# Mirrored sums and differences in a two-dimensional Fourier transform beside attention, one core of a Trainium2

## The chip, the cores and the metric

One core of one Trainium2 chip. The metric is the device time of one execution in microseconds; the kernel before was run three times. The core's engines are called PE (TensorE, matrix multiplication), ACT (ScalarE), DVE (VectorE), POOL (GpSimd) and SP (SyncE, which issues nearly all transfers here). They run side by side, each through its own fixed list of instructions in order, and wait for one another by semaphores. PSUM, where PE leaves its results, has eight banks.

## The reference

```python
B, S, D = 1, 2048, 448;  H = 16;  Dh = 28
g = sigmoid((x * gate_w).sum(-1))
qkv = x @ wqkv
p = softmax(q k^T * Dh ** -0.5)            # 16 heads, 2048 x 2048 each
a = (p v) @ wo
X = rfft2(x)                               # 2048 x 225 complex
b = irfft2(X * (w_r + 1j * w_i))
return g * a + (1 - g) * b
```

Both halves read the same x; everything is in bfloat16 outside, sums are in float32.

## The kernel before, in words

**Attention.** The 16 heads make four groups G of four. A group's queries are cut into four chunks of 512, so there are 16 chunks (CHUNKS gives their order). A chunk has 16 *packs*: one key tile of 128 keys, 512 queries, four heads. A pack's four units are scores of 128x512, each one matmul with a contraction of 32 (rows of the array, one strip a head). Two ways lead from scores to probabilities:

- ACT takes two units at a time from two-bank tiles psA and psB and writes exp into P, a ring of 20 units (line 901). The first few packs go into VS instead.
- DVE takes a unit from a psX bank and makes the bits of a bfloat16 power of two out of it by an addition in int16 (line 930). The result is a coarse exponential. From it DVE makes three more versions with other offsets (line 936), and all four are multiplied with the values, so that their errors cancel. Such a pack has four value products instead of one.

A value product is four matmuls side by side, each on 32 columns of the array, added up in psV over a whole chunk. When a chunk is done, DVE empties psV (line 1512) and the next opens.

**Fourier part.** `fft1` (lines 1380 to 1396) transforms over 128 rows: for each of 16 row tiles t and four column blocks c of 112, one matmul with the tokens as weights and R1 (128 columns) as the moving operand; four such fill a bank, DVE evicts it into U (line 1393). `fft2` (lines 1415 to 1470) does the rest for 16 blocks g of frequencies: f2 multiplies U with Bd, the cosine and sine table over the 448 columns of x (four blocks c of 112, each 452 columns wide, added up in one bank); f3 applies the twiddle table; POOL multiplies with the filter; i1 begins the way back. `fft3` does i2, `final` adds both halves. Bd's tile is reused for wo afterwards (line 1028). All these matmuls, and the projections, are cut by `mmc` into 32-column pieces that run side by side; only `fft1` and the transposes use the whole array.

**Order.** No engine's order is written out by hand. `Plan` is a small simulation in the program that builds the kernel: each operation has an engine, a cost and what it depends on, and `pe_step` (line 640) picks at each moment what PE does next by a score. Scores for ACT come first; other work is taken if it fits before ACT needs its next tile. Work of the Fourier part is offered in *units*, each with a time from which it may start and a time at which it is due, counted in chunks. `claim` (line 539) gives a pack to DVE when a bank, a free slot in VS and DVE's backlog allow it. So the number of packs that go to DVE comes out of the plan. If PE's work in the last 3.413 us, counted in columns (`load`), falls under z_hard, dense work is favoured or matmuls with zeros are put in (`zero`). An operation with port=True is one that the plan doesn't let POOL and DVE do at once. CFG holds the weights of all these choices, with one set of changes for each of 18 stretches: 16 chunks and what comes after (line 853); `run` looks up the set by `progress` (line 297).

Of the kernel before, what the change touches and what calls it, by code (L numbers as in the profile page):

```python
# [18 lines left out]
FP = F + 1  # L19
NG, NC = 4, 4  # L20
C = 112
# [20 lines left out]
def rfft_tables():  # L42
# [43 lines left out]
    bd = Bd.reshape(NC, C, 2 * FP).transpose(1, 0, 2)  # L86
# [72 lines left out]
class Plan:  # L159
# [116 lines left out]
    def run(self):  # L276
# [563 lines left out]
    def unit_run(self, u, o, t):  # L840
# [5 lines left out]

CFG = dict(
# [6 lines left out]
        0: dict(d_open=4, w_hungry=0, z_hard=3550, w_open=1.2),  # L854
        1: dict(tol=0),
        3: dict(tol=0.15),
        4: dict(ahead=2, tol=0.15),
        5: dict(v2_due=3.1, hungry=4, w_pv=0.6, tol=0.15),
        6: dict(hungry=4, prio_shift=3, tol=0.15),
        7: dict(w_pv=0.6, tol=0, v2_at=0.5, prio_shift=3),  # L860
        8: dict(w_pv=0.6, tol=0, prio_shift=3, z_hard=3550),
        9: dict(d_urg=1, d_chunks=0, w_due=4, prio_shift=3, z_hard=3550),
        10: dict(z_hard=3550, d_open=4),
        11: dict(z_hard=3550, g_at=[1.1, 4.3, 8.0]),
        12: dict(d_urg=1, ring_urg=8, z_hard=3550),
        13: dict(ring_urg=4, w_pv=0.2, prio_shift=3, z_hard=3550, d_urg=1, w_new=2.0, z_soft=3800, w_late=2),
        14: dict(w_open=0.2, prio_shift=3.5, ahead=1, w_late=2, w_pv=0.2, ring_urg=4, w_new=2.0, w_due=4, pv_min=2, z_soft=3800),
# [75 lines left out]
class Kernel:  # L943
# [36 lines left out]
    def tiles(self, ctx):  # L980
# [26 lines left out]
        self.R1T = self.cst[:, 460:588]  # L1007
# [101 lines left out]
    def loads(self):  # L1109
# [16 lines left out]
        self.d_r1 = self.dma(self.cst[:, 332:588], cs[:, 332:588], 5.0, [self.d_wv])  # L1126
        self.d_bd = self.dma(self.Bd[0:C, :, :], self.c_bd.ap(), 4.0, [self.d_r1])
# [252 lines left out]
    def fft1(self):  # L1380
        nc = self.nc
        self.o_u = []
        i = 0
        for tq in range(4):
            for c in range(NC):
# [7 lines left out]
                self.o_u.append(u.use("DVE", 0.61, lambda bank, e, c=c, tq=tq: nc.vector.tensor_copy(  # L1393
                    out=self.U[0:C, c, :, 4 * tq:4 * tq + 4, :],
                    in_=bank[0:C, :].rearrange("p (t g e) -> p g t e", t=4, g=NT))))
# [19 lines left out]
    def fft2(self):  # L1415
# [5 lines left out]
        for g in range(NT):  # L1421
# [4 lines left out]
            for c in range(NC):  # L1426
                u.mm(lambda bank, c=c, g=g: self.mmc(bank[:, 0:452], self.U[0:C, c, g, :, :].rearrange("p t e -> p (t e)"), self.Bd[0:C, c, :], c == 0, c == NC - 1), n=452, kind="bg", eff=0.875, deps=self.o_u + [self.d_bd])
# [182 lines left out]
```

## Time and profile before

| | us |
|---|---|
| median of three runs | 400.09 |
| lowest and highest | 399.91, 401.86 |
| the profiled execution | 400.49 |
| its span, first to last instruction | 398.7 |
| ACT, PE, DVE, POOL busy | 383.6, 386.0, 344.3, 126.9 |

The profile is one execution. A group's row gives line, engine, operation, what it writes and reads (partitions x elements), how often, then the busy time, the mean ns of one, and the engine's idle time before them with what ended it. Instructions of one engine overlap: the next can start before the last has ended, so the distance of two starts says more than the duration. A timeline row gives start, duration, and the instruction.

### The profile page before, as it was taken

Reading aid. Unit: us, or ns where it says so; the run is one execution under the profiler, and the core shown is the slowest. Engines: PE = TensorE matmul, PEld = TensorE weight load, DVE = VectorE, ACT = ScalarE, POOL = GpSimd, SP = SyncE. Lnnn points to the kernel's source line nnn. Section 1 sums busy time; section 2 is a strip of 40 time slices with the busy share of each in tenths; the row PEclk is TensorE's granted clock in tenths of the full one; section 3 lists DMA queues with packets and bytes.
Section 4 is the critical chain, followed back from the end, with each engine's and each line's share of the span. In section 5 each row is a group of like instructions: output and inputs, shape, how many; then the busy total and the mean of one; then the engine's idle time right before and its main releaser. Section 6 shows DMA issues by size and latency. Waiting matters only on the chain.

```text
span 398.7 us, 12653 instructions
## 1 busy us (share of the span) xinstructions
PE 386.0 (97%) x5221; PEld 134.9 (34%) x5221; DVE 344.3 (86%) x622; ACT 383.6 (96%) x424; POOL 126.9 (32%) x176
## 2 busy tenths in 40 slices
PE   8999999999999999999999999999999999999996
PEld 4444332223333322332332333333334332323233
DVE  3668999988887897898799797799998999999992
ACT  4898999999999999999999999999999999999993
POOL 1044214432333135525444534542436720101010
PEclk9999999999999999999999999999999999999999
DMA  8800022000121102120130112012100100001012
GB/s 250 181 31 5 2 28 58 13 19 3 37 70 34 40 3 66 32 77 20 24 100 19 56 37 58 14 42 74 36 29 2 29 3 25 30 27 50 26 53 71
DMA packets 24394, 17.69 MB, mean 44 GB/s; under 512 B 15731, under 2 KB 19744, under 8 KB 24336
## 3 DMA queue, kind: packets, MB, share of 16 engines
q1 hardware_dynamic: 23728, 16.69, 15.7%
q8 instruction: 41, 0.67, 0.7%
q10 hardware_dynamic: 608, 0.19, 0.3%
q14 instruction: 17, 0.14, 0.1%
HBM read 14.71 MB, written 1.97 MB: 42 GB/s over the span
## 4 chain that ended last, share of the span: by engine, by line
PE 46%; ACT 44%; issue 8%; DMA 1%; DVE 1%; ACTq 0%; DVEq 0%
ACT P L901 44%; PE psX L952 16%; PE psV L952 13%; PE psB L952 8%; PE psA L952 8%; DMA xtok<-in_A_x_dram 1%; PE psX L1202 1%; ACT VS L901 0%; DVE KT L1246 0%; DVE QT L1246 0%; ACT Vb L1227 0%; DVE Vb L1348 0%; PE psV L1202 0%; ACT sq L1556 0%; ACT sq L1237 0%
## 5 line engine op out<-in xcount | busy, mean ns | idle before, releaser
L901 ACT ACTIVATE P<-psB 128x1024 bf16<-128x1024 f32 x198 | 219.9, 1110 | 0.0
L901 ACT ACTIVATE P<-psA 128x1024 bf16<-128x1024 f32 x198 | 219.6, 1109 | 0.1
L930 DVE TENSOR_SCALAR VS<-psX 128x512 int16<-128x512 f32 x212 | 138.9, 681 | 17.3 <-PE psX L952 16.4
L936 DVE TENSOR_SCALAR VS<-VS 128x2048 int16<-128x2048 int16 x159 | 101.5, 689 | 0.4
L952 PEld LDWEIGHTS <-KT 32*128 32x128 bf16 (+1 forms) x1040 | 47.8, 91 | 145.3 <-issue 141.0
L952 PE MATMUL psB<-QT,KT 32*128 32x512 bf16 x406 | 79.2, 382 | 6.3 <-ACT P L901 5.0
L952 PE MATMUL psA<-QT,KT 32*128 32x512 bf16 x406 | 79.6, 383 | 0.9 <-DVE QT L1246 0.6
L952 PE MATMUL psV<-VS,Vb 128*32 128x512 bf16 x868 | 76.0, 385 | 0.1
L952 PE MATMUL psV<-P,Vb 128*32 128x512 bf16 x792 | 73.7, 385 | 0.0
L952 PE MATMUL psX<-QT,KT 32*128 32x512 bf16 x212 | 70.4, 383 | 0.0
L952 PEld LDWEIGHTS <-Vb 128*32 128x32 bf16 x1660 | 33.3, 94 | 57.0 <-issue 51.9
L1441 POOL TENSOR_TENSOR t<-FX,Wf 128x452 bf16<-128x452 f32 x32 | 31.8, 1013 | 56.1 <-PE psX L952 26.3
L1521 POOL TENSOR_TENSOR xtok<-osb,RB 128x512 bf16<-128x512 f32 x12 | 15.3, 1274 | 61.8 <-DMA RB<-rgd 47.6
L1184 POOL TENSOR_TENSOR sq<-QT 128x512 bf16<-128x512 bf16 x16 | 16.6, 1040 | 42.9 <-DVE QT L1266 17.3
L1495 POOL TENSOR_TENSOR UZ<-tab 128x225 bf16<-128x225 f32 (+1 forms) x32 | 17.7, 583 | 21.0 <-DVE VS L936 14.7
L952 PE MATMUL psX<-xT,Wk 112*32 112x512 bf16 x256 | 20.5, 383 | 0.0
L952 PE MATMUL psX<-xT,Wq 112*32 112x512 bf16 x240 | 20.0, 383 | 0.0
L1184 POOL TENSOR_TENSOR sq<-KT 128x512 bf16<-128x512 bf16 x12 | 12.5, 1040 | 22.6 <-DVE KT L1174 17.1
L952 PE MATMUL psX<-Bd,UZ 112*32 112x452 bf16 x256 | 19.6, 358 | 0.0
L1449 POOL TENSOR_TENSOR t<-t,t 128x226 bf16<-128x226 bf16 x32 | 17.9, 584 | 5.0 <-DVE VS L936 4.3
L952 PE MATMUL psX<-Wv,xT 112*32 112x113 bf16 (+1 forms) x512 | 19.4, 262 | 0.0
L952 PEld LDWEIGHTS <-xT 112*32 112x32 bf16 (+1 forms) x576 | 10.5, 96 | 9.0 <-issue 7.0
(105 smaller groups left out, 301.5 us busy)
## 6 DMA issues: line engine op xcount, KB each, us to landing
tab<-c_tab SPq DMA_DIRECT2D x16, 256.0 KB
RB<-rgd SPq DMA_DIRECT2D x60, 64.0 KB
xtok<-in_A_x_dram SPq DMA_DIRECT2D x4, 448.0 KB
out_dram<-ost SPq DMA_DIRECT2D x6, 224.0 KB
rs<-osb SPq DMA_DIRECT2D x60, 2.0 KB
Wf<-in_B_w_r_dram SPq DMA_DIRECT2D x31, 28.1 KB
Wf<-in_B_w_i_dram SPq DMA_DIRECT2D x31, 28.1 KB
Qf<-in_A_wqkv_dram SPq DMA_DIRECT2D x2, 294.0 KB
```

The costliest lines, as they stand in the source:

```text
L901: k.nc.scalar.activation(out=out, in_=k.psS[e["grp"]][:, 0:n, :], func=ACT.Exp, scale=LN2_128)
L930: k.nc.vector.tensor_scalar(out=k.VS[:, slot, 512 * h:512 * h + 512], in0=bank, scalar1=float(BITS0), scalar2=BITS_MIN, op0=ALU.add, op1=A ...
L936: k.nc.vector.tensor_scalar(out=k.VS[:, dst, :], in0=k.VS[:, src, :], scalar1=float(SHIFTS[v - 1]), scalar2=None, op0=ALU.add)
L952: self.nc.tensor.matmul(out, lhsT=lhsT, rhs=rhs, start=start, stop=stop, skip_group_check=True, **kw)
L1184: (self.nc.vector if e == "DVE" else self.nc.gpsimd).tensor_tensor(out=sq[:, :], in0=src, in1=src, op=ALU.mult)
L1202: nc.tensor.transpose(out=bb[0:C, 512 * ci + 128 * k:512 * ci + 128 * k + 128], in_=self.xtok3[:, 4 * b + k, C * c:C * c + C], identity=se ...
L1441: ts.append(pl.op("POOL", 1.07, lambda e, i=i, q=q: nc.gpsimd.tensor_tensor(out=self.t12[i][q][:, :].rearrange("p (r f) -> p r f", r=2), i ...
L1449: (nc.vector if e == "DVE" else nc.gpsimd).tensor_tensor(out=t1[:, FP * q:FP * q + FP], in0=t1[:, FP * q:FP * q + FP], in1=t2[:, FP - FP * ...
L1495: nc.gpsimd.tensor_tensor(out=z, in0=a, in1=b, op=ALU.subtract if q else ALU.add)
L1521: prev = pl.op("POOL", 1.3, lambda e, G=G, j=j: nc.gpsimd.tensor_tensor(out=self.ON[G][:, 512 * j:512 * j + 512], in0=self.osb[:, :], in1= ...
```

## The change

`fft1` uses that a cosine over the columns of x is the same at column d and at 448 - d, and a sine the opposite. It makes x[d] + x[448-d] and x[d] - x[448-d] while it transforms: each unit of matmuls is done once with the tokens and [R1, R1] and once, added in PSUM, with the mirrored tokens and [R1, -R1]. Of the 256 columns that a row tile gives, the first 128 are transforms of the sums, the other 128 of the differences. Of x's columns, 1 to 96 and 0 make one block of 97, and 97 to 224 another of 128. The mirrored tokens xr are written by four POOL copies that read backwards. f2 then multiplies the sums with the cosines and the differences with the sines alone: two blocks of 226 columns for each half, where four of 452 were. Each of `fft1`'s 16 units is 16 matmuls of 32 weights' columns and 256 moving columns, where it was four of 112 and 128; DVE evicts a unit in two pieces. The constants grow by -R1, and Bd's table is half as large. Columns 0 and 224 count half in the table, since they meet themselves.

The plan's set of changes is now looked up per quarter of a chunk (GRAIN), 72 sets, nearly all of them with new values.

```diff
@@ rfft_tables
-    bd = Bd.reshape(NC, C, 2 * FP).transpose(1, 0, 2)
+    i0 = np.concatenate([np.arange(1, 97), [0]])
+    i1 = np.arange(97, 225)
+    bd = np.zeros((128, 4, FP))
+    for blk in range(4):
+        i = (i0, i1)[blk % 2]
+        w = np.where((i == 0) | (i == D // 2), 0.5 if blk < 2 else 0.0, 1.0)
+        bd[:len(i), blk] = w[:, None] * Bd[i, blk // 2]
@@ small_tables
-    return np.concatenate([ident, np.zeros((128, 32)), selrow, sels, e, one, R1, R1.T], axis=1)
+    return np.concatenate([ident, np.zeros((128, 32)), selrow, sels, e, one, R1, -R1, R1.T], axis=1)
@@ Plan
-        self.cfgs = [dict(cfg, **cfg["seg"].get(i, {})) for i in range(18)]
+        self.cfgs = [dict(cfg, **cfg["seg"].get(i, {})) for i in range(18 * GRAIN)]
...
-            self.cfg = self.cfgs[int(self.progress())]
+            self.cfg = self.cfgs[int(GRAIN * self.progress())]
@@ CFG
+GRAIN = 4
...
-        0: dict(d_open=4, w_hungry=0, z_hard=3550, w_open=1.2),
-        1: dict(tol=0),
...
-        15: dict(prio_shift=3.5, w_open=0.2, w_late=1, w_pv=0.2, z_hard=3350, w_new=1.2, w_due=4, pv_min=2, z_soft=3800),
-        16: dict(sw_pen=1.5),
-        17: dict(z_soft=3800, w_new=1.2),
+        0: dict(d_open=4, w_hungry=0, z_hard=3550, w_open=1.2, tol=0.15),
+        1: dict(d_open=4, w_hungry=0, z_hard=3550, w_open=1.2),
+        2: dict(d_open=4, w_hungry=0, z_hard=3550, w_open=1.2, w_d=0.5, pv_min=2, tol=0),
+        3: dict(d_open=4, w_hungry=0, z_hard=3550, w_open=1.2, w_due=4, z_soft=3800),
+        4: dict(tol=0, d_open=2, prio_shift=3.5, z_hard=3350, d_urg=3, z_soft=4200),
...
+        9: dict(d_urg=3, pv_min=2, tol=0.06, z_hard=3350, d_chunks=0),
...
+        44: dict(d_urg=1, w_d=2.2, pv_min=2, z_soft=4200, z_hard=3250, w_late=1),
+        45: dict(w_d=2.2, pv_min=2, z_soft=4200, z_hard=3250, w_late=1, ring_urg=8, w_pv=0.2, d_open=2),
+        46: dict(w_d=2.2, pv_min=2, z_soft=3800, z_hard=3250, w_late=1, ring_urg=8, w_pv=0.2, d_open=2),
...
+        71: dict(z_soft=3800, w_new=1.2, ring_urg=8, ahead=2, w_open=1.2),
@@ tiles
-        self.R1T = self.cst[:, 460:588]
+        self.R1n = self.cst[:, 332:588]
+        self.R1T = self.cst[:, 588:716]
...
+        self.xr = self.Qf[:, 2 * NC * D:2 * NC * D + NT * 224].rearrange("p (t d) -> p t d", t=NT)
...
-        self.Bd = sb("Bd", [128, NC, 2 * FP])
+        self.Bdw = sb("Bd", [128, NG * D])
+        self.Bd = self.Bdw[:, 0:4 * FP].rearrange("p (c f) -> p c f", c=4)
...
-        self.Wo = self.Bd[:, :, :].rearrange("p c f -> p (c f)")[:, 0:NG * D].rearrange("p (g d) -> p g d", g=NG)
+        self.Wo = self.Bdw[:, :].rearrange("p (g d) -> p g d", g=NG)
@@ loads
-        self.d_r1 = self.dma(self.cst[:, 332:588], cs[:, 332:588], 5.0, [self.d_wv])
-        self.d_bd = self.dma(self.Bd[0:C, :, :], self.c_bd.ap(), 4.0, [self.d_r1])
+        self.d_r1 = self.dma(self.cst[:, 332:716], cs[:, 332:716], 5.0, [self.d_wv])
+        self.d_bd = self.dma(self.Bd[:, :, :], self.c_bd.ap(), 3.0, [self.d_r1])
@@ fft1
+        rev = [self.pl.op("POOL", 0.97, lambda e, b=b: nc.gpsimd.tensor_copy(out=self.xr[:, 4 * b:4 * b + 4, :], in_=self.xtok3[:, 4 * b:4 * b + 4, D - 1:D // 2 - 1:-1]),
+                          [self.d_x[b]], port=True, prio=4) for b in range(4)]
         i = 0
-        for tq in range(4):
-            for c in range(NC):
+        for tq in range(8):
+            for c in range(2):
                 u = self.pl.unit(0.4 + 0.06 * i, "f1", due=0.8 + 0.06 * i)
                 i += 1
 
                 def go(bank, c=c, tq=tq):
-                    for k in range(4):
-                        self.mm(bank[0:C, 128 * k:128 * k + 128], self.xtok3[:, 4 * tq + k, C * c:C * c + C], self.R1, True, True)
-                u.mm(go, n=128, count=4, eff=0.875, deps=[self.d_x[tq], self.d_r1])
-                self.o_u.append(u.use("DVE", 0.61, lambda bank, e, c=c, tq=tq: nc.vector.tensor_copy(
-                    out=self.U[0:C, c, :, 4 * tq:4 * tq + 4, :],
-                    in_=bank[0:C, :].rearrange("p (t g e) -> p g t e", t=4, g=NT))))
+                    for t in range(2):
+                        for f in range(2):
+                            x = self.xtok3[:, 2 * tq + t, :]
+                            r = self.R1n if f else self.R1[:, None, :].to_broadcast([128, 2, 128])
+                            for o in range(0, 128, 32):
+                                a = (97 if c else 1) + o
+                                w = x[:, 0:1] if c == 0 and o == 96 else self.xr[:, 2 * tq + t, a - 1:a + 31] if f else x[:, a:a + 32]
+                                out = bank[o:o + w.shape[-1], 256 * t:256 * t + 256]
+                                self.mm(out if f else out.rearrange("p (f n) -> p f n", f=2), w, r, f == 0, f == 1, pos=(0, o))
+                u.mm(go, n=256, count=4, kind="bg", eff=0.88, deps=[self.d_x[tq // 2], self.d_r1, rev[tq // 2]])
+
+                def ev(bank, e, c=c, tq=tq):
+                    n = 128 if c else 97
+                    for t in range(2):
+                        nc.vector.tensor_copy(out=self.U[0:n, 2 * c:2 * c + 2, :, 2 * tq + t, :],
+                                              in_=bank[0:n, 256 * t:256 * t + 256].rearrange("p (f g e) -> p f g e", f=2, g=NT))
+                self.o_u.append(u.use("DVE", 0.7, ev))
@@ fft2
-            for c in range(NC):
-                u.mm(lambda bank, c=c, g=g: self.mmc(bank[:, 0:452], self.U[0:C, c, g, :, :].rearrange("p t e -> p (t e)"), self.Bd[0:C, c, :], c == 0, c == NC - 1), n=452, kind="bg", eff=0.875, deps=self.o_u + [self.d_bd])
+            for c in range(4):
+                n = 128 if c % 2 else 97
+                u.mm(lambda bank, c=c, g=g, n=n: self.mmc(bank[:, FP * (c // 2):FP * (c // 2) + FP], self.U[0:n, 2 * (c % 2) + c // 2, g, :, :].rearrange("p t e -> p (t e)"), self.Bd[0:n, c, :], c % 2 == 0, c % 2 == 1), n=FP, kind="bg", eff=n / 128.0, deps=self.o_u + [self.d_bd])
```

More of the change, by code (lines that the diff above doesn't have):

```diff
@@ L853 @@
     seg={
-        0: dict(d_open=4, w_hungry=0, z_hard=3550, w_open=1.2),
-        1: dict(tol=0),
[L856 to L863, printed above, removed]
@@ new lines @@
+        6: dict(d_open=2),
+        7: dict(d_open=2, w_d=2.2),
+        8: dict(d_urg=3, pv_min=2, tol=0.06),
+        9: dict(d_urg=3, pv_min=2, tol=0.06, z_hard=3350, d_chunks=0),
+        10: dict(d_urg=3, pv_min=2, tol=0.06, w_due=1),
+        11: dict(w_hungry=4),
+        12: dict(tol=0.15, g_due=0.8, w_hungry=4, z_hard=3550),
+        13: dict(tol=0.15, g_due=0.8, w_hungry=4, z_hard=3550, prio_shift=3),
+        14: dict(tol=0.15, g_due=0.8, w_hungry=4, z_hard=3550, prio_shift=3, sw_pen=0.25),
@@ new lines @@
+        15: dict(tol=0.15, g_due=0.8, w_hungry=0, z_hard=3550, sw_pen=0.25, d_first=False, pv_min=3, hungry=1),
+        16: dict(ahead=1, tol=0.15, g_due=0.8, w_hungry=0, z_hard=3550, sw_pen=0.25, d_first=False, pv_min=3, hungry=1, d_open=4),
+        17: dict(ahead=2, tol=0.15, g_due=0.8, w_hungry=0, z_hard=3550, d_first=False, pv_min=3, hungry=1, prio_shift=3.5),
+        18: dict(ahead=2, tol=0.15, g_due=0.8, w_hungry=0, z_hard=3550, d_first=False, pv_min=3, hungry=1, w_d=1, max_ahead=5),
+        19: dict(ahead=2, tol=0.15, g_due=0.8, w_hungry=0, z_hard=3550, d_first=False, pv_min=3),
@@ new lines @@
+        20: dict(v2_due=3.1, w_pv=0.6, tol=0.15, g_due=0.8, w_hungry=0, z_hard=3550),
+        21: dict(v2_due=3.1, hungry=4, w_pv=0.6, tol=0.15, g_due=0.8, w_hungry=0, d_first=False, d_open=4),
+        22: dict(v2_due=3.1, hungry=4, w_pv=0.6, tol=0.15, g_due=0.8, w_hungry=0, d_first=False, d_open=4, ring_urg=8),
+        23: dict(v2_due=3.1, hungry=4, w_pv=0.6, tol=0.15, g_due=0.8, w_hungry=4, prio_shift=3.5),
+        24: dict(hungry=4, prio_shift=3.5, tol=0.15, g_due=0.8, w_hungry=0, w_due=4),
@@ new lines @@
+        25: dict(hungry=4, prio_shift=3.5, tol=0.15, g_due=0.8, w_hungry=0, w_due=4, d_open=2),
+        26: dict(hungry=4, prio_shift=3.5, tol=0.06, g_due=0.8, w_hungry=0, w_due=4, d_open=2, sh_max=2),
+        27: dict(hungry=4, prio_shift=3.5, tol=0.15, g_due=0.8, w_hungry=0, w_due=0.5, d_open=2, d_urg=3),
+        28: dict(g_due=0.8, w_hungry=0, prio_shift=3.5, w_due=4, d_open=2, z_soft=4200, d_first=False),
+        29: dict(g_due=0.8, w_hungry=0, prio_shift=3.5, w_due=4, d_open=2, z_soft=4200, d_first=False, sh_max=3),
@@ new lines @@
+        35: dict(g_due=0.8, prio_shift=3.5, z_soft=4200, d_first=False, w_hungry=2, d_urg=3),
+        36: dict(d_urg=3, d_chunks=0, w_due=4, prio_shift=3.5, z_hard=3550, z_soft=4200, g_due=0.8, ring_urg=4, d_first=False, w_hungry=2),
+        37: dict(d_urg=3, d_chunks=0, w_due=4, prio_shift=3.5, z_hard=3550, g_due=0.8, w_d=2.2),
+        38: dict(d_urg=3, d_chunks=0, w_due=0.5, prio_shift=3.5, z_hard=3550, g_due=0.8, w_d=1.4, w_hungry=2),
+        39: dict(d_urg=3, d_chunks=0, w_due=4, prio_shift=3.5, z_hard=3550, g_due=0.8, sh_max=3, pv_min=2, w_d=2.2, hungry=3),
@@ new lines @@
+        46: dict(w_d=2.2, pv_min=2, z_soft=3800, z_hard=3250, w_late=1, ring_urg=8, w_pv=0.2, d_open=2),
+        47: dict(w_d=2.2, pv_min=2, ring_urg=8, w_pv=0.2, d_open=2, w_new=2.0),
+        48: dict(w_d=2.2, pv_min=2, ring_urg=8, w_pv=0.2, d_open=2, hungry=4, sw_pen=1.5, max_ahead=5),
+        49: dict(w_d=2.2, pv_min=2, w_pv=0.6, d_open=2, tol=0),
+        50: dict(pv_min=2),
+        51: dict(w_new=2.4),
+        52: dict(ring_urg=4, w_pv=0.2, prio_shift=3.5, z_hard=3550, d_urg=1, w_new=2.4, z_soft=3800, w_late=0, pv_min=2, v2_at=1.2, ahead=6),
@@ new lines @@
+        53: dict(ring_urg=4, w_pv=0.2, prio_shift=3.5, z_hard=3550, d_urg=1, w_new=2.4, z_soft=3800, w_late=0, pv_min=2, v2_at=1.2, sw_pen=2),
+        54: dict(ring_urg=4, w_pv=0.2, prio_shift=3.5, z_hard=3550, d_urg=1, w_new=2.0, z_soft=3800, w_late=0, pv_min=2, v2_at=1.2, sw_pen=2, max_ahead=5, w_due=0.5),
+        55: dict(ring_urg=4, w_pv=0.2, prio_shift=3.5, z_hard=3550, d_urg=1, w_new=2.0, z_soft=3800, w_late=0, pv_min=2, v2_at=1.2, w_due=0.5),
+        56: dict(w_hungry=0, prio_shift=3.5, w_new=2.0, max_ahead=5, w_due=0.5, tol=0),
@@ new lines @@
+        57: dict(w_hungry=0, prio_shift=3.5, w_new=2.0, max_ahead=5, w_due=0.5, tol=0.15),
+        58: dict(w_hungry=4, prio_shift=3.5, w_new=2.0, max_ahead=5, w_due=0.5, tol=0.15),
+        59: dict(w_hungry=0, prio_shift=3.5, w_new=2.0, max_ahead=5, w_due=0.5, tol=0.15, sw_pen=1.5),
+        60: dict(w_hungry=0, prio_shift=3.5, w_new=2.0, max_ahead=5, w_due=0.5, tol=0.15, w_pv=1.8),
+        61: dict(w_hungry=0, prio_shift=3.5, w_new=2.0, max_ahead=5, w_due=0.5, tol=0.15, ahead=2),
+        62: dict(w_hungry=0, prio_shift=3.5, w_new=2.0, max_ahead=5, w_due=0.5, ahead=2, w_late=1, hungry=3, z_soft=4200),
@@ new lines @@
+        63: dict(w_hungry=0, prio_shift=3.5, ahead=2),
+        64: dict(sw_pen=1.5, ring_urg=8, w_hungry=0, ahead=2, w_open=1.2),
+        65: dict(sw_pen=1.5, ring_urg=8, w_hungry=0, ahead=2, w_open=1.2),
+        66: dict(sw_pen=1.5, ring_urg=8, w_hungry=0, ahead=2, w_open=1.2),
+        67: dict(sw_pen=1.5, ring_urg=8, w_hungry=0, ahead=2, w_open=1.2),
+        68: dict(z_soft=3800, w_new=1.2, ring_urg=8, ahead=2),
+        69: dict(z_soft=3800, w_new=1.2, ring_urg=8, ahead=2, w_open=1.2),
```

15 lines of the change are left out of this document (11 added, 4 removed).

## The prediction

> **What bounds the kernel now.** I read the totals first, then a table of busy time by stage, then ScalarE (ACT) and TensorE (PE) instruction by instruction.
>
> ```profile
> L901 ACT ACTIVATE P<-psB 128x1024 bf16<-128x1024 f32 x198 | 219.9, 1110 | 0.0
> L901 ACT ACTIVATE P<-psA 128x1024 bf16<-128x1024 f32 x198 | 219.6, 1109 | 0.1
> L930 DVE TENSOR_SCALAR VS<-psX 128x512 int16<-128x512 f32 x212 | 138.9, 681 | 17.3 <-PE psX L952 16.4
> L936 DVE TENSOR_SCALAR VS<-VS 128x2048 int16<-128x2048 int16 x159 | 101.5, 689 | 0.4
> ```
>
> The first two are exponentials; the last two are DVE's way to the same result. By stages (columns: the stretch and its length, then busy time of PE, weight loads, DVE, ACT, POOL, the granted clock, DMA):
>
> ```profile
> 0.00:35.00 35.00, 32.72 (x579) 17.00 (x583) 19.24 (x46) 26.38 (x33) 5.27 (x12) 1.00 0.52 132
> 35.00:62.00 27.00, 26.36 (x282) 10.61 (x271) 26.24 (x49) 27.00 (x30) 8.36 (x27) 1.00 0.14 23
> 62.00:90.00 28.00, 27.55 (x354) 7.79 (x352) 25.47 (x46) 28.00 (x32) 10.94 (x11) 1.00 0.07 21
> 90.00:268.00 178.00, 176.60 (x2394) 57.05 (x2386) 154.01 (x271) 178.00 (x195) 70.16 (x80) 1.00 0.16 41
> 268.00:389.00 121.00, 117.07 (x1519) 39.37 (x1517) 116.73 (x204) 121.00 (x132) 32.15 (x48) 1.00 0.11 32
> 389.00:398.70 9.70, 5.74 (x120) 3.05 (x112) 2.57 (x10) 3.26 (x7) 0.00 (x0) 1.00 0.22 73
> sum 398.70, PE 386.04 PEld 134.87 DVE 344.26 ACT 383.64 POOL 126.88; mean PE 64.34 PEld 22.48 DVE 57.38 ACT 63.94 POOL 21.15
> ```
>
> Over the span of 398.7 us PE and ACT look equally full, so the sums don't say which one sets the end. But from 35 to 389 us ACT is never idle, and its instructions follow one another like this:
>
> ```profile
> 12.65 1.02 ACT L901 ACTIVATE VS<-psA 128x1024 bf16<-128x1024 f32 x1 [1.10 <-PE psB L952]
> ...
> 31.44 1.40 ACT L901 ACTIVATE P<-psB 128x1024 bf16<-128x1024 f32 x1
> 34.35 0.21 ACT L1358 ACTIVATE ge<-glog 128x16 f32<-128x16 f32 x1 [1.51 <-DVE glog L1334]
> 34.71 1.02 ACT L901 ACTIVATE P<-psA 128x1024 bf16<-128x1024 f32 x1
> ...
> 387.32 1.03 ACT L901 ACTIVATE P<-psA 128x1024 bf16<-128x1024 f32 x1
> 388.22 1.04 ACT L901 ACTIVATE P<-psB 128x1024 bf16<-128x1024 f32 x1
> ```
>
> One exponential starts 0.90 us after the one before (387.32 to 388.22; the 1.1 us durations overlap). The work is 1024 units of 128x512 scores. 212 of them, or 53 packs of four, go to DVE (L930), and with three variants each that makes the 159 of L936. The other 812 go to ACT by twos: 406 exponentials, the 396 above and ten early ones into VS. From 12.65 to 388.22 are 375.6 us, and 405 steps of 0.905 are 366.5. The other 9.1 us are other ACT work and one wait, 31.44 to 34.71, of 2.4 us. So the time is a head of 12.7, **0.905 us an exponential**, 9.1 us of breaks, and an end of 10.5. An edit gains what it takes off that sum, and the large term falls only when a pack goes to DVE: two exponentials fewer, **1.81 us a pack**.
>
> **What stands against more packs.** DVE is busy 96% from 268 to 389 us, but 87% from 90 to 268, with 24.0 us idle. There PE is the tight one (176.6 of 178). This is a PE sequence from that stretch:
>
> ```profile
> 202.83 0.39 PE L952 MATMUL psA<-QT,KT 32*128 32x512 bf16 x2
> 202.84 0.39 PE L952 MATMUL psX<-QT,KT 32*128 32x512 bf16 x1
> 203.15 0.62 PE L952 MATMUL psX<-tab,t 128*32 128x256 bf16 x16
> 203.75 0.39 PE L952 MATMUL psB<-QT,KT 32*128 32x512 bf16 x2
> 204.07 0.61 PE L952 MATMUL psV<-VS,Vb 128*32 128x512 bf16 x8
> 204.66 0.39 PE L952 MATMUL psA<-QT,KT 32*128 32x512 bf16 x2
> 204.98 0.57 PE L952 MATMUL psX<-Bd,UZ 112*32 112x452 bf16 x8
> 205.48 0.39 PE L952 MATMUL psX<-QT,KT 32*128 32x512 bf16 x1
> ```
>
> Between two score pairs (about 0.905 us) lie 0.32 us of scores (202.83 to 203.15) and a visit to 32-column work: two 512-column passes take 0.59 (204.07 to 204.66), four 256-column passes 0.60. A pass is four matmuls side by side. Eight matmuls last 0.61 and one 0.39, so a second pass adds 0.22 us per 512 columns; the visit is then 0.44 of columns and 0.15 of turning round. One slot thus holds 0.905 - 0.32 - 0.15 = 0.43 us of columns. A pack moved to DVE takes two slots away (0.87) and adds three value passes (0.66): **1.5 us of PE** if its four scores ride beside a pair, as the one at 202.84 does, and 2.8 if all four stand alone at 0.32 each.
>
> **The second transform.**
>
> ```profile
> L952 PE MATMUL psX<-Bd,UZ 112*32 112x452 bf16 x256 | 19.6, 358 | 0.0
> ```
>
> 256 matmuls are 64 passes of 452 columns. Two of them and the turn take 0.50 us (204.98 to 205.48), so one is 0.17 to 0.19. They stay 64 but get 226 columns: 64 x 226 columns at 0.22 us per 512 is **6.2 us of PE saved**, in the stretch from 90 to 268.
>
> **The first transform.**
>
> ```profile
> 38.26 0.43 PE L952 MATMUL psX<-cst,xtok 128*112 128x128 bf16 x4
> 38.62 0.39 PE L952 MATMUL psB<-QT,KT 32*128 32x512 bf16 x2
> ...
> L1393 DVE CAST UZ<-psX 112x512 bf16<-112x512 f32 x16 | 10.5, 679 | 0.5 <-PE psX L952 0.4
> ...
> L1341 DVE CAST Vb<-psX 128x336 bf16<-128x336 f32 x16 | 8.0, 501 | 1.1 <-PE psX L952 1.1
> ```
>
> A unit now is four whole-array matmuls of 128 columns, 0.36 us in its slot (38.26 to 38.62). After, it is 16 matmuls in four passes of 256 columns, the shape of the 0.60 us visit at 203.15. Sixteen units cost 16 x (0.60 - 0.36) = 3.8 us more if each has a visit to itself. If each shares one, the turn falls away (0.44 against 0.36): 1.3 more. I take 2.5, the middle: a unit of 0.44 fills a slot (0.43) by itself, but a value pass is often due there. The Trainium skill (TensorEngine Tiling (Array Packing), Key Properties) says that changing the tiling mode drains the array. The 0.15 us of turning agrees, and by the rule the old whole-array unit paid a turn each time while the new one pays none beside value passes, which would be the 1.3.
>
> DVE evicts 32 pieces of 256 columns instead of 16 of 512. Through 679 ns at 512 and 501 at 336 a line gives 420 at 256: 32 x 0.420 - 16 x 0.679 = 2.6 us more, in 35 to 62, where DVE has 0.8 idle. That is half a pack (4 x 0.681 + 3 x 0.689 = 4.8 us) lost there.
>
> **The mirrored copies** are new: four POOL copies of 128x896, read backwards.
>
> ```profile
> 5.61 0.95 POOL L1153 COPY Wq<-Qf 112x112 bf16<-112x112 bf16 x4 [5.17 <-DMA Qf<-in_A_wqkv_dram]
> 20.06 1.04 POOL L1184 TENSOR_TENSOR sq<-QT 128x512 bf16<-128x512 bf16 x1 [13.50 <-PE psX L952]
> ...
> 8.65 0.60 PE L952 MATMUL psX<-xT,Wq 112*32 112x512 bf16 x8
> ```
>
> Four copies of 112 columns take 0.95, so 896 columns are at most 1.9 us by their rate, and at least the 0.24 of one such copy; I take 1.3, nearer to the rate. POOL idles 13.5 us before 20.06 and the first transform was at work at 38, so all four (1.0 to 7.6 us) are hidden. The first transform now waits for them, and behind its units on PE stand the next scores: a copy late by more than that idle time would stop ACT. Behind one of them waits POOL's Wq copy: 6.56 would become at most 8.5, and PE reads Wq at 8.65. Without that cover the head slips one for one, at most 1 us. On SP's queue the two constant loads stay two: the one with R1 grows by half, the Bd one shrinks, no stage waits for them; 0. The later wo load and memset into Bd's tile keep their place.
>
> **The order.** The planner's parameters now change every quarter of a chunk. What that moves no row shows. Bounds: nothing, or DVE's 24.0 idle us filled, five packs (4.8 each) in all together with the PE gain, plus the 2.4 us wait. Below nothing too: see the clock.
>
> **The sum.** PE freed: 6.2 less 1.3 to 3.8 is 2.4 to 4.9 us; at 2.8 to 1.5 a pack, 0.9 to 3.3 packs, middle two. The lost half pack in 35 to 62 is DVE's and is made up where DVE idles. For finer planning I add one pack, at the low side of its bounds because every window to 268 lacks PE before DVE. **Three packs, 56 in all, 400 exponentials: 6 x 0.905 = 5.4 us.** The profiled run took 400.5 us, 1.8 around its span and 0.4 over the median shown (400.1, inside its 399.9 to 401.9): 395.1. With one to five packs: 398.7 to 391.4.
>
> **Rivals.**
>
> (a) The PE time is freed and no pack goes over, since a pack also needs a bank, a variant slot and DVE at the right moment. For it: DVE at 96% in the last third. Against: 24 us idle before. 404 to 408 exponentials, 398.7 to 402.3; middle 400.5.
>
> (b) The short passes cost more than their columns. The worst the 0.60 us visit allows is all 0.16 of its turn spread over the four passes, 0.04 each; 64 new passes are 2.6 us, which leaves 0 to 2.3 us of the PE gain, none or one pack: 398.7 to 400.5, middle 399.6. Against: the 0.59 visit of two passes has the same turn. The Trainium skill (TensorEngine Tiling (Array Packing), Instruction Overhead) states about 60 cycles of overhead a matmul and speaks against this change: 192 more matmuls would be some 4.8 us by it, an estimate, and the PE gain gone: 400.5. The two visits, 8 and 16 matmuls in 0.59 and 0.60, do not show it.
>
> (c) **Slower: the array is starved and its clock drops.** Some 6 us of columns less, and nothing put in their place, can leave a stretch with little running; the plan holds a floor of counted columns (z_hard), and the change sets it at its lowest (3250 or 3350) in five quarters spread over the run, where before only one chunk had 3350.
>
> ```profile
> L952 PE MATMUL psV<-ost 128*128 128x448 bf16 x13 | 4.7, 516 | 1.2 <-DVE ost L1129 1.2
> ```
>
> 448 columns, most of them at the start, took 516 ns, while the second transform's 452 take 358: a slow array exists, but the granted clock of the stages is 1.00 throughout. At half rate a slot's 0.22 + 0.43 of columns double, 0.65 us lost per 0.905. Three packs are paid back after 5.4 / 0.65 = 8 slots, and the change is slower by 0.5% after 7.4 / 0.65 = 11, some 18 us at half rate; 20 us (13 slots) give 395.1 + 8.4 = 403.5. The Trainium skill (TensorE: Matmul & The Clock Gate, Part 1) says that an idle window of about 3.4 us halves the clock; by that rule one lapse costs few us. Against: the floor is counted for the new shapes too.
>
> (d) The doubled first transform starves the value product in 35 to 62: the ring of P fills and ACT waits as at 31.44. The 3.8 us of PE and 2.6 of DVE unhidden, with at most two packs elsewhere: 400.5 + 6.4 - 3.6 = 403.3. It decides from about five us of wait.
>
> (e) More than five packs, or five and shorter breaks. Six are 12 x 0.905 = 10.9 us off, 389.6; with the 2.4 us wait gone as well, 387.2. For it: nothing but the idle 24 us of DVE, which five packs fill.
>
> **How the numbers follow.** Forecast 0.66, of which 0.06 is the one-pack end; (a) 0.10, (b) 0.04, (c) 0.07, (d) 0.07, (e) 0.06. A measurement here can tell about 0.5%, 2.0 us: under 398.1 is faster, over 402.1 slower. Faster: 0.60 + 0.06 + 0.05 of (a), where the 2.4 us wait also goes = 0.71. Slower: 0.07 + 0.07 + 0.01 of (a) = 0.15. Same: the rest, 0.14. The range 391.0 to 402.0 leaves out (c), (e) and part of (d); the forecast's own is 391.4 to 398.7.
>
> **What would show it.** L901 near 400 in all, still 0.905 apart; L930 near 224 and L936 near 168; DVE's idle time in 90 to 268 down by some 14 us; Bd,UZ still 256 but 226 columns wide; some 256 matmuls of xtok and the mirrored columns (in Qf) where 64 were, four passes in 0.44 to 0.60; 32 evictions near 420 ns; POOL's four copies of 0.8 to 1.9 us before 20 us; first exponential still near 12.7. Wrong if the exponentials are 404 or more, if their steps grow (gaps in 35 to 62), or if the granted clock falls under 1.00 in a stage.

## The result, and the profile after

The kernel after took 396.49 us (median of six runs, 395.82 to 398.30), the one before beside it 400.53 (399.91 to 401.86). The ratio is 0.990, 95% interval 0.9875 to 0.9929: about 1% faster. The profiled execution took 396.5 us, of which 394.4 is its span. The rows below are from its page of costliest groups and answer to those of lines 901, 930 and 936 before (in the prediction).

```profile
L963 ACT ACTIVATE P<-psB 128x1024 bf16<-128x1024 f32 x196 | 218.4, 1114 | 0.3
L963 ACT ACTIVATE P<-psA 128x1024 bf16<-128x1024 f32 x196 | 217.8, 1111 | 0.3 <-ACT P L963 0.2
L992 DVE TENSOR_SCALAR VS<-psX 128x512 int16<-128x512 f32 x220 | 144.0, 683 | 10.6 <-PE psX L1014 9.7
L998 DVE TENSOR_SCALAR VS<-VS 128x2048 int16<-128x2048 int16 x165 | 107.5, 694 | 0.5
```

220 units, 55 packs, go to DVE now: two more than before. Exponentials are 392 and the ten early ones, 402 instead of 406. The next fence is ACT's timeline at the start, at the place of the old wait, and at the last exponential.

```profile
12.87 1.02 ACT L963 ACTIVATE VS<-psA 128x1024 bf16<-128x1024 f32 x1 [1.10 <-PE psB L1014]
...
28.46 0.65 ACT L1292 ACTIVATE Vb<-psX 128x64 bf16<-128x64 f32 x1
28.57 1.40 ACT L963 ACTIVATE P<-psB 128x1024 bf16<-128x1024 f32 x1
29.64 1.23 ACT L963 ACTIVATE P<-psA 128x1024 bf16<-128x1024 f32 x1
...
383.87 1.02 ACT L963 ACTIVATE P<-psA 128x1024 bf16<-128x1024 f32 x1
384.77 1.03 ACT L963 ACTIVATE P<-psB 128x1024 bf16<-128x1024 f32 x1
```

The step is 0.90 us as before. The span can be taken apart by these starts; a *break* is what the time between two exponentials has beyond 0.905 us (sums are of unrounded values):

| us | before | after | difference |
|---|---|---|---|
| head, to the first exponential | 12.7 | 12.9 | +0.2 |
| steps of 0.905 | 405: 366.5 | 401: 362.9 | -3.6 |
| breaks between exponentials | 9.0 | 9.0 | 0.0 |
| from the last exponential to the end | 10.5 | 9.6 | -0.8 |
| span | 398.7 | 394.4 | -4.3 |

The old wait is gone. It stood behind the exponential at 31.44, which follows ACT's small instruction into Vb; at that place the two exponentials are now 1.07 us apart (28.57 to 29.64) where 3.27 were (31.44 to 34.71). But the breaks together are as long as before. Up to 35 us they fell from 4.0 to 2.5 us, after 268 us they grew from 1.9 to 3.0, and between they grew by 0.4, all in small ones.

Busy time by stages (stretch, its length, then PE, weight loads, DVE, ACT, POOL, granted clock, DMA), and below it DVE's and PE's part in tile VS alone (PE, DVE, ACT), before and after:

```profile
35.00:62.00 27.00, 27.00 (x480) 10.87 (x478) 24.72 (x60) 27.00 (x32) 7.53 (x26) 1.00 0.10 13
...
90.00:268.00 178.00, 176.39 (x2480) 59.27 (x2477) 165.81 (x292) 177.92 (x195) 73.69 (x84) 1.00 0.17 46
268.00:385.00 117.00, 113.19 (x1481) 37.60 (x1478) 113.53 (x199) 116.46 (x127) 29.20 (x44) 1.00 0.09 26
385.00:394.40 9.40, 5.91 (x124) 3.02 (x116) 2.94 (x11) 3.63 (x7) 0.00 (x0) 0.95 0.22 75
```

```profile
35.00:62.00 27.00, 4.41 (x48) 14.08 (x22) 0.00 (x0) 1.00 0.14 23
90.00:268.00 178.00, 32.19 (x372) 105.49 (x163) 0.00 (x0) 1.00 0.16 41
```

```profile
35.00:62.00 27.00, 4.41 (x48) 12.27 (x19) 0.00 (x0) 1.00 0.10 13
90.00:268.00 178.00, 36.17 (x408) 116.46 (x179) 0.00 (x0) 1.00 0.17 46
```

From 90 to 268 us DVE's idle time fell from 24.0 to 12.2 us, and 11.0 of these 11.8 are work on VS: 2.3 packs at 4.8 us. The units that DVE began say the same more sharply. Up to 62 us they are 14 before and 14 after, then 17 and 17 to 90 us, 94 and 102 to 268, and 87 and 87 from there on: both packs were won in the stretch in which the second transform runs. From 35 to 62 us DVE does 1.8 us less for packs (10 units where 13 were), but three more units come before 35 us.

The clock was 1.00 until 385 us. The 0.95 of the last stage comes from its last 2.4 us: from 392 us on PE has no instruction left, and the granted clock there is 0.80.

PE's timeline at two units of the first transform, and at a whole product of the second:

```profile
38.61 0.29 PE L1014 MATMUL psX<-cst,xtok 128*32 128x256 bf16 x4
38.73 0.28 PE L1014 MATMUL psX<-cst,Qf 128*32 128x256 bf16 x4
38.84 0.28 PE L1014 MATMUL psX<-cst,xtok 128*32 128x256 bf16 x4
38.95 0.28 PE L1014 MATMUL psX<-cst,Qf 128*32 128x256 bf16 x4
39.17 0.39 PE L1014 MATMUL psB<-QT,KT 32*128 32x512 bf16 x2
39.49 0.39 PE L1014 MATMUL psX<-cst,xtok 128*32 128x256 bf16 x5
...
39.94 0.39 PE L1014 MATMUL psV<-VS,Vb 128*32 128x512 bf16 x4
...
191.07 0.58 PE L1014 MATMUL psX<-Bd,UZ 97*32 97x226 bf16 x16
191.58 0.39 PE L1014 MATMUL psX<-QT,KT 32*128 32x512 bf16 x1
```

A unit of the first transform with a visit to itself takes 0.56 us (38.61 to 39.17), one that shares its visit 0.45 (39.49 to 39.94). Eleven of the 16 have a visit to themselves. All together they take 8.9 us of PE, counted from the first matmul of a unit to the next other one, where they took 5.6 before. The whole second product of a block, 16 matmuls, takes 0.51 with its turn; before, half of one took 0.50. Over all 16 blocks it took 16.3 us before and 8.5 after. The other new pieces, from the groups by shape:

```profile
L1472 DVE CAST UZ<-psX 97x256 bf16<-97x256 f32 x16 | 6.0, 418 | 0.1
L1472 DVE CAST UZ<-psX 128x256 bf16<-128x256 f32 x16 | 6.0, 416 | 0.0
...
L1449 POOL COPY Qf<-xtok 128x896 bf16<-128x896 bf16 x4 | 3.7, 935 | 6.0 <-DMA xtok<-in_A_x_dram 6.0
```

### The profile page after: what moved, and what is told of

Its sections match the earlier page's. It is cut to its first block, busy times and chain, and to the rows that moved or that the text cites. A ratio compares the mean times of both kernels' runs of the same rounds, so it can differ in the third digit from the quotient of the medians.

```text
span 394.4 us, 13102 instructions
## 1 busy us (share of the span) xinstructions
PE 382.2 (97%) x5432; PEld 134.9 (34%) x5432; DVE 353.3 (90%) x651; ACT 380.8 (97%) x421; POOL 131.2 (33%) x180
## 4 chain that ended last, share of the span: by engine, by line
PE 59%; ACT 33%; issue 5%; DMA 1%; DVE 0%; SPq 0%; ACTq 0%
ACT P L963 30%; PE psX L1014 20%; PE psV L1014 18%; PE psA L1014 10%; PE psB L1014 10%; DMA xtok<-in_A_x_dram 1%; ACT VS L963 1%; ACT sq L1636 0%; PE psX L1267 0%; ACT sq L1302 0%; ACT xT L1274 0%; SPq L1169 0%; DVE KT L1311 0%; DVE QT L1311 0%; PE psV L1267 0%
## 5 line engine op out<-in xcount | busy, mean ns | idle before, releaser
L992 DVE TENSOR_SCALAR VS<-psX 128x512 int16<-128x512 f32 x220 | 144.0, 683 | 10.6 <-PE psX L1014 9.7
L998 DVE TENSOR_SCALAR VS<-VS 128x2048 int16<-128x2048 int16 x165 | 107.5, 694 | 0.5
L1014 PEld LDWEIGHTS <-KT 32*128 32x128 bf16 x1040 | 47.2, 91 | 140.2 <-issue 136.7
L1014 PE MATMUL psB<-QT,KT 32*128 32x512 bf16 x402 | 78.4, 382 | 5.0 <-ACT P L963 4.0
L1014 PE MATMUL psA<-QT,KT 32*128 32x512 bf16 x402 | 78.8, 383 | 1.2 <-ACT P L963 0.6
L1014 PE MATMUL psV<-VS,Vb 128*32 128x512 bf16 x900 | 79.7, 385 | 0.0
L1014 PE MATMUL psV<-P,Vb 128*32 128x512 bf16 x784 | 72.0, 384 | 0.0
L1249 POOL TENSOR_TENSOR sq<-QT 128x512 bf16<-128x512 bf16 x16 | 16.6, 1041 | 29.8 <-PE psX L1014 12.1
L1529 POOL TENSOR_TENSOR t<-t,t 128x226 bf16<-128x226 bf16 x32 | 18.1, 583 | 14.5 <-DVE VS L998 13.1
L1014 PEld LDWEIGHTS <-xT 112*32 112x32 bf16 (+1 forms) x576 | 10.6, 95 | 10.4 <-issue 8.1
L1546 DVE CAST Qf<-psX 113x512 bf16<-113x512 f32 x16 | 10.9, 683 | 1.5 <-PE psX L1014 1.3
```

The source lines that it names most:

```text
L992: k.nc.vector.tensor_scalar(out=k.VS[:, slot, 512 * h:512 * h + 512], in0=bank, scalar1=float(BITS0), scalar2=BITS_MIN, op0=ALU.add, op1=A ...
L998: k.nc.vector.tensor_scalar(out=k.VS[:, dst, :], in0=k.VS[:, src, :], scalar1=float(SHIFTS[v - 1]), scalar2=None, op0=ALU.add)
L1014: self.nc.tensor.matmul(out, lhsT=lhsT, rhs=rhs, start=start, stop=stop, skip_group_check=True, **kw)
L1249: (self.nc.vector if e == "DVE" else self.nc.gpsimd).tensor_tensor(out=sq[:, :], in0=src, in1=src, op=ALU.mult)
L1529: (nc.vector if e == "DVE" else nc.gpsimd).tensor_tensor(out=t1[:, FP * q:FP * q + FP], in0=t1[:, FP * q:FP * q + FP], in1=t2[:, FP - FP * ...
L1546: self.o_q.append(u.use("DVE", 0.61, lambda bank, e, g=g: nc.vector.tensor_copy(out=self.Qv[0:FC, :, :, 8 * g:8 * g + 8], in_=bank[0:FC, : ...
```

## The experiments

Every time is a median, and every ratio is to the kernel before, run beside it on the same chip (400.0 to 400.1 us).

**1. Freed PE time without a new order.** In the kernel before, f2 alone, costed in the plan as before, so that the order stays. Half of the products are left out (`U[...]` and `...` shorten the line):

```diff
-  self.mmc(bank[:, 0:452], self.U[...], self.Bd[0:C, c, :], c == 0, c == NC - 1), ...
+  self.mmc(bank[:, FP * (c % 2):FP * (c % 2) + FP], self.U[...], self.Bd[0:C, c, FP * (c % 2):FP * (c % 2) + FP], c < 2, c >= 2), ...
```

> The kernel before, its order of instructions kept, but each f2 pass moves 226 columns instead of 452 (each half of the result gets two of the four column blocks, so half of the second transform's products are left out). Theory: the end is set by the number of exponentials, and PE's columns count only where the plan turns them into packs; 406 exponentials stay, so 400.5 us, within 1 us. Rival: PE is the bound by itself, and 64 x 226 columns less are 6.2 us less: 394.

Measured: 399.98 us, ratio 0.9996 (0.9986 to 1.0005). Its first and last exponential, and the stretch of f2:

```profile
12.06 1.02 ACT L901 ACTIVATE VS<-psA 128x1024 bf16<-128x1024 f32 x1 [1.10 <-PE psB L952]
...
387.57 1.04 ACT L901 ACTIVATE P<-psB 128x1024 bf16<-128x1024 f32 x1
```

```profile
90.00:268.00 178.00, 173.68 (x2391) 59.76 (x2385) 154.20 (x273) 178.00 (x196) 70.75 (x81) 1.00 0.16 41
```

375.5 us between the two starts, 375.6 before. PE has become 2.9 us less busy there, and nothing else moved. Halving the product is worth nothing by itself: in this order PE was not the bound.

**2. The freed PE time given back.** In the kernel after, in the same order (the plan doesn't count them), a pass with zero weights beside each f2 pass (shortened in the same way):

```diff
-  self.mmc(bank[...], self.U[...], self.Bd[0:n, c, :], c % 2 == 0, c % 2 == 1)
+  out = bank[...]
+  self.mmc(out, self.U[...], self.Bd[0:n, c, :], c % 2 == 0, False)
+  for o in range(0, 128, 32):
+      self.mm(out[o:o + 32], self.zw[0:n], self.Bd[0:n, c, :], False, c % 2 == 1, pos=(0, o))
```

> The kernel after, its order kept, but beside each f2 pass of 226 columns a second one of as many columns with weights of zero, so that PE gets back the 6.2 us that the change took from f2. Theory: PE is tight between 90 and 268 us, 402 exponentials stay, but the steps between them grow: 396.5 + 3 to 6 = 399.5 to 402.5 us. Rival: the freed PE time was not needed for the two packs, PE had slack: 396.5, within 1 us.

Measured: 400.09 us, ratio 0.9999 (0.9989 to 1.0009). ACT at its ends, and the stretch of f2:

```profile
12.44 1.02 ACT L963 ACTIVATE VS<-psA 128x1024 bf16<-128x1024 f32 x1 [1.09 <-PE psB L1014]
...
388.47 1.03 ACT L963 ACTIVATE P<-psB 128x1024 bf16<-128x1024 f32 x1
```

```profile
90.00:268.00 178.00, 177.43 (x2695) 63.18 (x2692) 162.07 (x285) 176.40 (x191) 72.90 (x83) 1.00 0.17 43
```

The same 402 exponentials now stretch over 376.0 us instead of 371.9, and ACT, which was idle for 0.1 us from 90 to 268, is idle for 1.6 there; the other delays are longer steps that the overlap of durations hides. All of the 4.1 us lie in this stretch, where the breaks grew from 2.7 to 6.8. So the 6.2 us of PE work cost 4.1 us between the exponentials, 3.6 by the medians, and the rest found room. Runs 1 and 2 together: in the order with 55 packs PE has no slack for the old product, and in the old order the smaller product does nothing. Whether another order could hold 55 packs with the old product is a question that run 2 can't answer, since it keeps the order.

**3. The packs taken away.** `nd_max=53` in the kernel after.

> The kernel after with at most 53 packs for DVE (nd_max=53), as many as before; all else as planned. Theory: four exponentials more, 4 x 0.905 = 3.6 us: 400.1 us, so nearly the whole gain is two packs. Rival: the gain comes from elsewhere (breaks, end, transforms): 396.5 to 397.5.

Measured: 399.17 us, ratio 0.9986 (0.9972 to 1.0000).

```profile
14.32 1.02 ACT L963 ACTIVATE VS<-psA 128x1024 bf16<-128x1024 f32 x1 [1.10 <-PE psB L1014]
...
389.88 1.03 ACT L963 ACTIVATE P<-psB 128x1024 bf16<-128x1024 f32 x1
```

Between first and last are 375.6 us, 3.7 more than after: four steps, as the theory has it. It is a clean comparison: PE does the same matmuls in the same order up to 372 us in both kernels, and the breaks are 9.0 us in both. The time is one less than the 400.1 expected. Against the kernel after, the medians differ by 2.7 us; but each was measured beside runs of its own of the kernel before, and by the two ratios (0.9986 and 0.990) it is 3.4 us. What is left of the gain without the packs, about 1 us, is of the size of the shorter end (9.3 us here, 10.5 before).

**4. One part at a time.** The new transform with the 18 old sets, and the old transform with the 72 new ones.

> The change without its second part: the new first and second transform, planned by the 18 sets of the kernel before. Theory: PE time freed brings about two packs with any good plan: 55 packs, 396 to 398 us. Rival: the old sets fit the old transform alone, and the packs come only with sets fitted to the new one: 53 packs or fewer, 400 us or more.

> The change without its first part: the old first and second transform, planned by the 72 sets of the kernel after. Theory (from the run with the new transform and the old sets, which was slower): sets and transform fit only each other; no more than 53 packs, 400 us or more. Rival: the finer sets are what gains: 54 or 55 packs, 396.5 to 399 us.

Measured: 404.83 us (ratio 1.0118, 1.0090 to 1.0146) and 404.88 us (1.0140, 1.0106 to 1.0174). Each part alone is slower than the kernel before. The first of them has this row:

```profile
L937 DVE TENSOR_SCALAR VS<-psX 128x512 int16<-128x512 f32 x208 | 136.0, 682 | 14.3 <-PE psX L959 13.8
```

208 units are 52 packs, one fewer than before, and the second kernel has 52 too: with more PE time, but sets that were fitted to another load, the plan gives DVE less. The theory put down for the first kernel (any good plan will do) fell, and its rival held; the theory for the second held. The lost pack is 1.8 us of the 4.7 and 4.9 us by which they are slower. About as much is the longer end: from the last exponential to the end are 12.3 and 12.1 us, where the kernel before has 10.5.

**5. How tight is the fit?** One cost in the plan changed: 0.70 us for an eviction unit of `fft1` became 0.71, and then 0.83, what the two instructions were measured to take (2 x 0.417).

> The kernel after with one number of the plan changed: an eviction unit of the first transform is costed at 0.71 us instead of 0.70. The work is the same. Theory: the plan is fitted to its exact costs, so the order from there on changes, and packs are lost: 53 packs, 399 to 405 us. Rival: a hundredth of a microsecond changes nothing: 55 packs, 396.5 us.

> The kernel after with the eviction unit of the first transform costed in the plan at 0.83 us, two instructions at the 0.417 that they were measured to take, instead of 0.70. The work is the same. Theory: the 72 sets fit the order that they were searched for and no other, so a truer cost loses packs: 51 packs, 410 exponentials, 404 to 409 us. Rival: a truer plan runs better: 396.5 or less.

Measured: 406.07 us (ratio 1.0152, 1.0135 to 1.0168) and 405.73 us (1.0140, 1.0107 to 1.0173). The transforms and the scores to be computed are the same; only the order differs, and with it the number of packs.

```profile
L992 DVE TENSOR_SCALAR VS<-psX 128x512 int16<-128x512 f32 x204 | 134.0, 682 | 15.9 <-PE psX L1014 15.4
```

51 packs in the second. The first keeps 53, as expected, but lies above the 405 expected at most: the four exponentials more are 3.6 of the 9.6 us by which it is behind the kernel after, and the larger part is elsewhere. 4.3 us are its end (14.0 us; its last matmul starts 10.1 us behind the last exponential, in the kernel after 5.8 us), and 2.2 are longer breaks; its head was 0.3 shorter in the profile. So a hundredth of a microsecond in a cost takes away more than twice what the whole change gains, though the cost is not that exact itself: 0.83 adds two durations that overlap, and by DVE's busy time (11.8 us for the 16 units) one is 0.74.

**6. No sets at all.** All stretches planned by the base weights, new transform and old.

> The kernel after with all 72 sets empty, so that the new transform is planned by the base weights alone. To be read against the old transform planned in the same way. Theory: the freed PE time (2.4 to 4.9 us) is not turned into packs by itself: within 2 us of the old transform's run. Rival: it is worth two packs whatever the plan: 3.6 us faster than the old transform's run.

> The kernel before with all 18 sets empty: the old transform planned by the base weights alone. Both theories: slower than 400.1, since the sets are gone, some 52 packs, 402 to 406 us.

Measured: 408.57 and 408.76 us, both with ratio 1.0216 (1.0170 to 1.0262 and 1.0189 to 1.0244). Both have 52 packs, and their breaks are 15.2 and 17.2 us. Without fitted sets the new transform is worth nothing that can be measured. The old one was expected at 406 at most. In six of the eight executions the mean granted clock was under 1.00, down to 0.986; at 1.00 the two kernels took 406.7 and 407.1, once each (more on this in the last section).

**7. Sets fitted anew.** For each transform 72 sets were searched for a shorter plan, starting from the 18 old sets, with the same effort; and the sets of the kernel after were searched further.

> The kernel before with 72 sets that were searched for its own transform, starting from its 18: the finer order alone, with sets that fit. 53 packs. Theory: without PE time freed no pack is gained, 406 exponentials stay: 399.5 to 400. Rival: fitted quarters alone gain what the change gains: 396.5.

> The new transform with 72 sets that were searched with the same effort, starting from the 18 of before. 53 packs. Theory: time goes by exponentials, 406 of them as before, so 400 us within 1.5, 3.6 us behind the kernel after, whose sets hold 55. Rival: the transform gains by itself once sets fit it: 397 or less.

> The kernel after with its 72 sets searched further for a shorter plan; the work and the 55 packs stay. Theory: with the packs the same, only breaks and the end can shrink, so 396.5 less at most half a microsecond. Rival: the search is worth another pack: 394.7 or less.

Measured: the old transform 400.56 us (ratio 1.0013, 1.0003 to 1.0022), the new one 399.08 (0.9978, 0.9969 to 0.9987), the refined kernel 395.95 (0.9900, 0.9885 to 0.9915). Both newly fitted kernels have 53 packs (212 units in their profiles) and the time that goes with it (the old transform's is 0.6 above the 400 expected at most); they differ by about the end after the last exponential, 10.4 us and 9.2. Finer sets alone gave the old transform no pack, and a new search gave the new transform none either. The refined sets keep 55 packs and are the fastest kernel here, but not clear of the kernel after. That these searches found no better sets doesn't prove there are none: whether some sets give the old transform 55 packs stays open.

The profiled executions of all these kernels, by the parts of the sum (us; head left out):

| run | kernel | packs | exponentials | breaks | end |
|---|---|---|---|---|---|
| | before | 53 | 406 | 9.0 | 10.5 |
| | after | 55 | 402 | 9.0 | 9.6 |
| 1 | before, half of f2 | 53 | 406 | 9.0 | 10.5 |
| 2 | after, f2 twice | 55 | 402 | 13.1 | 9.6 |
| 3 | after, 53 packs | 53 | 406 | 9.0 | 9.3 |
| 4 | new transform, old sets | 52 | 408 | 9.5 | 12.3 |
| 4 | old transform, new sets | 52 | 408 | 10.5 | 12.1 |
| 5 | cost 0.71 | 53 | 406 | 11.2 | 14.0 |
| 5 | cost 0.83 | 51 | 410 | 10.6 | 10.2 |
| 6 | new transform, no sets | 52 | 408 | 15.2 | 11.2 |
| 6 | old transform, no sets | 52 | 408 | 17.2 | 10.1 |
| 7 | old transform, fitted | 53 | 406 | 9.2 | 10.4 |
| 7 | new transform, fitted | 53 | 406 | 9.3 | 9.2 |
| 7 | after, refined | 55 | 402 | 8.6 | 10.0 |

So a poor order costs not only packs: the breaks range over 8.6 us and the end over 4.8.

## Why the prediction was right, by its own steps

**The sum of the time.** The step held in every profile (median 0.904 or 0.905 us), and so did two exponentials a pack. That the other terms stay held for the kernel after and for runs 1 and 3, and not for every plan (table above). Runs 2 and 3 put the freed PE time and the packs back one by one, and each took most of the gain with it.

**The second transform.** 6.2 us of PE freed were forecast; 7.8 were found (16.3 to 8.5). The rest fits the turns, which the sum left out: 41 visits became 29, and 12 turns of 0.15 us are 1.8. Predicted was that it counts only through packs: run 1 shows that (0.0 us by itself), run 2 shows that the order with 55 packs needs it (4.1 us come back as time), and the units counted by stretch show that both packs are won where it runs.

**The first transform.** 0.60 us alone and 0.44 shared were forecast; 0.56 and 0.45 were found. As 11 of 16 units stood alone, the whole is 3.2 us more (5.6 to 8.9, rounded), within the 1.3 to 3.8 and above the 2.5 taken. DVE's evictions 420 ns, found 416 to 418; but two overlap, and DVE's busy time for them grew by 1.3 us (10.5 to 11.8), not 2.6. The half pack that this was to cost in 35 to 62 seems to be there (0.4), but not for the reason given: up to 62 us DVE began 14 units as before, and from 35 to 62 it was idle for 2.3 us, more than the 0.8 before, while PE had no idle time at all (27.00 of 27.00).

**The mirrored copies** took 0.94 us each, between the bounds (0.24 to 1.9) and below the 1.3 taken. They are hidden; what they did to DVE was not foreseen (last section).

**The number of packs** is the term that was mis-sized: three were forecast, two came, 3.6 us instead of 5.4 in the steps. The PE account alone gave 0.9 to 3.3, middle two, and two came; with the sizes found, 7.8 less 3.2, it gives 1.6 to 3.1. The third was added for the finer order, by its bounds, and it isn't there: finer sets by themselves gave no pack (runs 4 and 7). The order's part is of another kind than the prediction had it. It is not an extra gain beside the transform but the condition for the transform's gain. Rival (a), PE time freed and no pack gained, is what the new transform did with sets fitted to it anew (53 packs, run 7), and with the old sets it lost a pack (run 4). So that the account's middle came true exactly is in part luck: several plans with the same freed time did not hold the two packs, and this one did. That the time came within 1.4 us of the forecast is helped by the end, whose 0.8 us the sum did not have.

**The breaks** were not to change in the likeliest case; in sum they did not, though the 2.4 us wait did go. The end became 0.8 us shorter, which no step had. It goes with the order, from 9.2 to 14.0 us in the table; what makes it shorter here, these runs don't settle.

**Rivals.** (b), short passes with overhead: 16 matmuls of 226 columns in 0.51 us with the turn leave no room for it. (c), the clock: 1.00 up to 385 us, at the lowered floors too. By its letter the prediction's sign of being wrong did show, 0.95 in the last stage; but that is where PE had finished, and it cost nothing that the rows show. In run 6 the clock did drop (last section). (d), starvation in 35 to 62: ACT was busy for 27.00 of 27.00. (e): no.

## What to carry to other kernels

Where one engine runs without a pause, count its instructions before anything else: work saved on another engine is worth what it lets you take off that count, and a run that saves the work without changing the order shows at once whether it is worth anything by itself. When a plan was fitted by search, even a small change of cost can throw the fit away (run 5), so a new algorithm has to be judged with sets fitted to it, and beside it the old one fitted with the same effort. The freed time and the fit can both be needed; test each by putting it back alone. And take every run's time apart: a plan that is worse can have lost packs, breaks or the end.

## What had not been expected of the hardware

**POOL's copies slow DVE's.** The first mirrored copy delays POOL's Wq copies, so that four DVE copies at the start of the program now run beside POOL's. The kernel before, then after:

```profile
5.27 0.49 DVE L1153 COPY Wk<-Qf 112x112 bf16<-112x112 bf16 x4 [0.76 <-DMA Qf<-in_A_wqkv_dram]
```

```profile
6.01 1.18 DVE L1218 COPY Wk<-Qf 112x112 bf16<-112x112 bf16 x4 [0.87 <-DMA Qf<-in_A_wqkv_dram]
```

```profile
5.53 0.93 POOL L1449 COPY Qf<-xtok 128x896 bf16<-128x896 bf16 x1 [5.09 <-DMA xtok<-in_A_x_dram]
6.40 0.96 POOL L1218 COPY Wq<-Qf 112x112 bf16<-112x112 bf16 x4
```

0.49 us became 1.18, the same copies: 0.19 to 0.20 us each before, when POOL's began as DVE's ended (its Wq copies start at 5.61), and now 0.50 for the first, beside the mirrored copy, and 0.32 for the three beside the Wq copies. The first ends at 6.51, 0.05 us behind the mirrored copy (6.46); in the run with 53 packs it is 6.40 behind 6.35. POOL's copies are no slower (0.95 and 0.96 us for the four into Wq). The plan keeps its marked operations of the two engines apart, and these DVE copies are not marked. The Trainium skill (GPSIMD Engine Reference, Specifications) says that POOL shares its SBUF interfaces with DVE and contends with DVE instructions in a two-port mode; these rows fit that, though none shows which mode the copies run in. Whether it cost time isn't shown: from the first transposes to the first exponential are 7.35 us here (5.52 to 12.87) and 7.83 before (4.82 to 12.65), but there the transposes were the slower ones of the next paragraph.

**The head varies by two microseconds.** The first transposes of PE in the kernel before, in the kernel after, and in the run with 53 packs, the last two with the same order at that point:

```profile
4.82 1.95 PE L1202 MATMUL psX<-cst,xtok 128*112 128x128 bf16 x16
```

```profile
5.52 1.10 PE L1267 MATMUL psX<-cst,xtok 128*112 128x128 bf16 x16 [0.95 <-DMA xtok<-in_A_x_dram]
7.41 0.65 PE L1267 MATMUL psX<-cst,xtok 128*112 128x128 bf16 x8 [0.22 <-DMA xtok<-in_A_x_dram]
```

```profile
5.41 1.96 PE L1267 MATMUL psX<-cst,xtok 128*112 128x128 bf16 x16 [0.71 <-DMA xtok<-in_A_x_dram]
8.28 1.06 PE L1267 MATMUL psX<-cst,xtok 128*112 128x128 bf16 x8
```

The same transposes took 1.10 or 1.96 us, and the first exponential came at 12.87 or 14.32. That profiled execution took 401.0 us, against a median of 399.2. The traces' records of the granted clock begin only at 4.3 us in the kernel after, at 9.6 in the run with 53 packs, and at 6.8 in the kernel before; ahead of the first record the views print 1.00 for want of one. In run 1 the record begins among the transposes, at 5.45 us: up to there they start 0.11 us apart, from there on 0.06. In the profiles on record the first exponential lies between 12.0 and 14.3 us, and the spans of single profiles have to be compared from the first exponential on. The Trainium skill (TensorE: Matmul & The Clock Gate, Part 1) has the array start at half its clock and be released after a window of activity that doesn't begin with the program, so that the moment differs from run to run; these rows agree with it.

**A lapse of the clock, in another plan.** In the old transform without sets (run 6) the granted clock is half for 10.2 us:

```profile
348.00:352.60 4.60, 4.00 (x42) 1.20 (x34) 4.17 (x7) 4.60 (x6) 0.00 (x0) 1.00 0.14 50
352.60:356.00 3.40, 3.40 (x26) 0.54 (x22) 2.58 (x5) 2.71 (x3) 0.00 (x0) 0.50 0.03 2
```

It ends at 362.8 us. Just ahead of it PE is busy for 4.00 of 4.60 us, so a busy share near 90% doesn't rule a lapse out. Eight steps between exponentials, from 352.29 to 363.82, take 11.53 us where 7.24 would do: 4.3 us lost. Rival (c) had reckoned 0.65 us lost for each slot of 0.905, and 10.2 us at 1.555 a slot are 6.6 slots, 4.3 us. So the price in (c) was right, but in the kernel after no lapse came before PE's work was done.
